# Capacity-routed mixture of experts on one core: second-layer weights by column halves, routings ended earlier, a third expert's tokens turned by DMA

## The chip, the core and the metric

The kernel runs on one core of a Trainium2 chip. The metric is the device time of one execution in microseconds (us), as the median of several runs. The core has five engines with a queue of instructions each: PE (TensorE, matmuls), DVE (VectorE), ACT (ScalarE), POOL (GpSimd) and SP (SyncE, which here issues transfers). An engine takes its instructions in the order of its queue, and one that has to wait holds up all that stand behind it.

## What is computed

The output of an attention is the input of a mixture of experts:

```python
scores = cap * np.tanh(scale * (q @ k.T) / cap)        # 8 x 12 heads, seq 448, dim 64
attn = softmax(scores); attn_out = attn @ v            # -> x: 3584 tokens x 768
logits = x @ w_gate                                    # 3584 x 8
cap = N // E                                           # 448
for idx in np.argsort(-logits.flatten()):
    tok, e = idx // E, idx % E
    if assigned[tok] >= 0 or counts[e] >= cap: continue
    assigned[tok] = e; counts[e] += 1
for e in range(E):
    mask = assigned == e
    out[mask] = np.maximum(x[mask] @ w1[e], 0.0) @ w2[e]   # 768 -> 1024 -> 768
```

All is fp32. Each expert ends with exactly 448 tokens. Which expert fills up first, and with which tokens, is known only when the logits are there, so the kernel finds it step by step: one routing for each expert.

## The kernel before

**Parts.** Attention and the first routing take the first 376 us or so. Then eight experts follow one another, in the order in which they fill up; "expert p" below means the p-th of that order, from 0. While PE works on expert p, the routing of expert p+1 or p+2 runs beside it on the other engines, in pieces.

**One expert.** The first layer (`ffn1`, f = 0 to 7) makes one block of 128 hidden columns at a time, the second (`ffn2`, u = 0 to 7) one tile of up to 128 tokens (t = u % 4) and one half of 384 output columns (hf = u // 4). The products of fp32 numbers are made from three matmuls: both factors are split into a high part (rounded) and a low part (the rest), and high x high, high x low and low x high are added. So a block of the first layer has 6 x 3 = 18 matmuls, a tile of the second has 24 (the last tile 16). That makes 144 + 176 = 320 matmuls for an expert. Each of them is one **tick**: the kernel counts them as it writes the program, and by this count it decides where all other work goes. "Tick 100 of expert 4" is behind the hundredth matmul of that expert. A call with `work={3:...}` puts its piece behind the third matmul of its block.

**The splits.** `split1(p,f)` splits a block of w1, `split2` a block of w2, both by `cut`: ACT rounds the high part (L758), POOL subtracts for the low part (L762). w1 blocks go out two blocks ahead, behind matmul 3 of a block of the first layer. Two blocks of w2 rows are loaded as one piece of 768 KB (`load2`, three buffers) and split in two column halves, one behind matmul 11 of each block of the first layer.

**The routing.** It is one Python generator; `step()` runs it to its next `yield`, and the number that is yielded says after how many ticks the next piece is written into the program. A negative number means: at that absolute tick (`LK` in `phases0`). For expert p it looks for the threshold in three searches, A, B and C (`select`): in each step, DVE (L504) and ACT (L501) count the values below several thresholds, a small matmul (L508) adds the counts over the partitions, and DVE picks the next thresholds. L567 sums the result over partitions. `finalise` turns thresholds to token lists: comparisons and a running count on DVE (L605 to L611), matmul L617 and L618 (prefix sums), one-hot patterns on DVE (L621 to L635), matmul L639, DVE again (L642, L644), matmul L647, and the list of token numbers. Its small matmuls stand in PE's queue among those of the expert, at the ticks that the yields make.

**The tokens of the next expert.** As soon as a list is there, POOL gathers the 448 rows of x from DRAM (L790). For experts 1 and 2 PE turns them, four transposes for each of six pieces (`xtr`, L806), and ACT and DVE split the result (`cutx`). From the third expert on (`FT`), DMA turns them: 26, 34, 42 and 50 ticks behind the gather, ACT rewrites a tile as two int16 planes (`planes`, L812) and sends it to DRAM, and behind the second and the fourth SP issues a DMA transpose (L816) of the first 256 and of the other 192 tokens. `cutt` splits these in four pieces: high parts on ACT (L822), low parts on DVE (L823).

**The order** is written out by hand: for every engine it is the order in which the Python code makes the calls. Nothing moves at run time.

Of the kernel before, what the change touches and what calls it, by code (L numbers as in the profile page):

```python
# [325 lines left out]
YL=[]  # L326
LK=(0,0,145,132,132,132,132,100); FT=3
ACF=1
# [4 lines left out]
class Routing:  # L333
# [188 lines left out]
    def search(s,wp,turned=()):  # L522
        nc=s.nc; v=nc.vector
# [12 lines left out]
        v.scalar_tensor_tensor(q,s.V["VA"][:,:s.NV],s.tA,vb,op0=ALU.subtract,op1=ALU.add)  # L536
        if s.cur>FT: yield max(0,306-s.place()-4)
        s.R=[]
# [62 lines left out]
    def finalise(s,wp,L,update):  # L601
        nc=s.nc; T=s.T; NC=s.NC; v=nc.vector
# [10 lines left out]
        if s.cur>=FT: s.early(s.cur,ei)  # L613
        yield 8 if s.cur==1 else 30 if s.cur==7 else 18 if s.cur>=FT else 12
        ps=s.psum()
# [19 lines left out]
        v.tensor_tensor(oi,oh,wide(s.idc),op=ALU.mult)  # L635
        yield 18
        ps=s.psum()
# [46 lines left out]

W1B=4; W2B=3
def ffn_all(nc, tc, ctx, rt, xs, xz, w1, w2, out, ident, E, wp, deferred, xctx, gen):
# [4 lines left out]
    res=rt.results  # L691
    hint=[0]; now=[0]
    def step():
        h=next(gen,0)
        hint[0]=max(-h-now[0],4) if h<0 else h
# [11 lines left out]
    m=0  # L707
# [33 lines left out]
    def load1(p,i,gate=None):  # L741
# [5 lines left out]
        raw[p,1,i]=t  # L747
    def load2(p,i,gate=None):
        if p>=E: return
        e=expert(p)  # L750
        t=ws.tile([128,2,DM],F32,name="w2r",bufs=W2B)
        if gate is not None: nc.gpsimd.tensor_copy(t[0:1,0,0:1],gate)
        nc.sync.dma_start(t,w2[bass.ds(e,1),i*256:i*256+256,:].rearrange("o (c p) d -> p (o c) d",p=128))
        raw[p,2,i]=t
    def cut(key,r,shape,name,bufs,eng=None,view=lambda t:t,use=lambda t:t):
# [8 lines left out]
    def split1(p,f,eng=None):  # L764
        if p>=E: return
        cut((p,1,f),raw[p,1,f],[128,DC,128],"w1",3,eng)
    def split2(p,hf,i):
        if p>=E: return
        r=raw[p,2,i]
        src=r[:,:,hf*HD:hf*HD+HD]  # L770
        view=use=lambda t:t.rearrange("p (o d) -> p o d",o=2)
        cut((p,2,hf,i),src,[128,2*HD],"w2",8,None,view,use)
    def early(p,ei):
# [43 lines left out]
    def cutt(p,k,c0,c1):  # L817
        newx(p)
        o,n=((0,256),(256,192))[k]
        h,l=(t[:,c0:c1,o:o+n] for t in xgT[p])  # L820
        x=xgp[k][:,c0*n:c1*n].rearrange("p (c t) -> p c t",c=c1-c0)
        nc.scalar.activation(h,x,AF.Copy)  # L822
        nc.vector.tensor_tensor(l,x,h.bitcast(F32),op=ALU.subtract)  # L823
    def cutx(p,c,ps):
        h,l=xgT[p]
# [86 lines left out]
    for p in range(E):  # L912
        lastp=p==E-1; cur[0]=p
        for f in range(FC):
            if f==0: load2(p,2)
            if f+W1B-1<FC and (p==0 or f+W1B-1>=W1B): load1(p,f+W1B-1) if (p,1,f+W1B-1) not in raw else None
            if f==(3 if p else 4): load2(p,3)
            work={}
            if f+2<FC and (p,1,f+2) not in spl: work[3]=[lambda: split1(p,f+2)]
            at={f:[(11,f%2,f//2)] for f in range(FC)}  # L920
            if p==0: at={1:[(11,0,0)],2:[(11,1,0)],3:[(11,0,1)],4:[(11,1,1)],5:[(11,0,2)],6:[(3,1,2),(11,0,3)],7:[(3,1,3)]}
            for n,hf,i in at.get(f,()): work[n]=[lambda hf=hf,i=i: split2(p,hf,i)]
            if p==1 and f==0: work[1]=[lambda: xtr(1,4)]; work[4]=[lambda: xtr(1,5)]
            ffn1(p,f,work)
# [12 lines left out]
        for u in range(8):  # L937
# [8 lines left out]
            if p<1 and u==7: wk={15:[lambda: xtr(1,3)]}  # L946
            if p+1>=FT and not lastp:
                for m,k,c in {6:[(5,0,0),(9,1,0),(12,0,3),(15,1,3)]}.get(u,()): wk[m]=wk.get(m,[])+[lambda k=k,c=c: cutt(p+1,k,c,c+3)]
            ffn2(p,u%4,u//4,(CL if p<1 else CP)[u] if p+1<FT else [],wk)
# [60 lines left out]
```

## Time and profile before

| | |
|---|---|
| time, median of 3 runs | 895.49 us (894.23 to 896.71) |
| the profiled execution's own time | 898.33 us |
| its span in the profile | 896.6 us |
| granted TensorE clock | 1.0 of full speed |
| DMA traffic | 136.84 MB |

The starts of the experts in the trace (first matmul of L855) and the time to the next one, or to the last output:

| expert | first matmul at | first matmul of L883 at | to the next expert |
|---|---|---|---|
| 1 | 448.22 | 479.49 | 66.6 |
| 2 | 514.84 | 545.13 | 62.6 |
| 3 | 577.47 | 611.35 | 66.2 |
| 4 | 643.69 | 674.79 | 63.5 |
| 5 | 707.14 | 738.28 | 62.4 |
| 6 | 769.57 | 799.29 | 62.6 |
| 7 | 832.13 | 861.32 | |

The profile's timeline has one row for each instruction: start in us from the start of the span, duration, engine, line of the code, what it writes and reads, sizes, and in brackets how long its engine sat idle before it and which instruction ended that. Where rows alike stand together it joins them ("x3"). Matmuls overlap, so the distance from one start to the next is what a matmul takes, not its duration.

### The profile page before, as it was taken

To read this page: it belongs to the slowest core of one execution; us is meant where nothing else is said; L and a number is where in the kernel's file an instruction comes from. 1 tells how busy PE (TensorE), PEld (TensorE's weight loads), DVE (VectorE), ACT (ScalarE), POOL (GpSimd) and SP (SyncE) were. 2 spreads that over 40 slices of the span, in tenths; PEclk is the share of its full clock that TensorE was granted. 3 is DMA by queue.
4 is the path that set the end of the run, shared out by engine and by line. 5 is a ranking of instruction groups with operands and counts; after the bars stand their busy time and mean duration, and the time that the engine had idled before them with its cause. 6 is when DMAs were issued, how large, how long until landed. Compare 5 with 4: busy or idle time off the path is not lost.

```text
span 896.6 us, 17418 instructions
## 1 busy us (share of the span) xinstructions
PE 862.6 (96%) x6222; PEld 631.5 (70%) x6222; DVE 613.7 (68%) x2012; ACT 584.8 (65%) x836; POOL 352.7 (39%) x506
## 2 busy tenths in 40 slices
PE   6899999999999997899999999899999999999997
PEld 3333444444333335788989989789989889989997
DVE  3788988989888888777787777677777774260210
ACT  6998898889899957274382573683673764535521
POOL 7100000000000008574584394394592683773841
PEclk9999999999999999999999999999999999999999
DMA  8799999997994007760923623944945927928701
GB/s 119 115 135 140 130 177 169 136 166 109 213 174 83 1 14 255 228 219 8 319 80 100 227 80 113 274 142 128 275 127 161 298 70 207 305 59 236 252 10 53
DMA packets 321463, 136.84 MB, mean 153 GB/s; under 512 B 252288, under 2 KB 303232, under 8 KB 320864
## 3 DMA queue, kind: packets, MB, share of 16 engines
q1 hardware_dynamic: 312304, 106.59, 54.0%
q0 software_dynamic: 4656, 22.02, 7.2%
q10 hardware_dynamic: 4416, 7.11, 2.4%
q8 instruction: 49, 0.80, 0.4%
q14 instruction: 38, 0.31, 0.1%
HBM read 97.15 MB, written 31.65 MB: 144 GB/s over the span
## 4 chain that ended last, share of the span: by engine, by line
PE 69%; issue 12%; POOL 5%; DVE 5%; DMA 4%; SPq 2%; ACT 2%; POOLq 0%; ACTq 0%; DVEq 0%
PE psH L855 20%; PE psH L883 15%; PE psA L189 12%; PE psS L148 10%; PE psM L206 4%; DMA xg<-xz 2%; PE psS L153 2%; SPq L92 2%; POOL w1l L762 2%; POOL out_dram L868 1%; DVE cmpD L504 1%; PE psM L37 1%; DVE es L165 1%; POOL xg L790 1%; DMA k<-in_k_dram 1%
## 5 line engine op out<-in xcount | busy, mean ns | idle before, releaser
L883 PE MATMUL psH<-w2h,hh 128*128 128x384 f32 x896 | 243.0, 340 | 0.0
L883 PE MATMUL psH<-w2l,hh 128*128 128x384 f32 x512 | 174.2, 340 | 0.0
L154 ACT ACTIVATE e<-psS 128x896 f32<-128x896 f32 x168 | 147.4, 909 | 30.8 <-PE psS L148 18.2
L883 PEld LDWEIGHTS psH<-w2h,hh 128*128 128x128 f32 x896 | 162.1, 188 | 0.2
L159 ACT ACTIVATE e<-e,bias 128x1792 f32<-128x1792 f32 (+2 forms) x74 | 147.3, 1991 | 2.0
L855 PE MATMUL psH<-xgh,w1h 128*128 128x448 f32 x384 | 143.4, 373 | 0.3 <-ACT xgh L827 0.3
L855 PE MATMUL psH<-xgh,w1l 128*128 128x448 f32 x384 | 141.3, 368 | 0.0
L855 PE MATMUL psH<-xgl,w1h 128*128 128x448 f32 x384 | 141.0, 368 | 0.1
L148 PE MATMUL psS<-tq,tk 64*64 64x448 f32 x1152 | 129.6, 544 | 7.8 <-DVE tq L133 3.5
L189 PE MATMUL psA<-e,nv 64*64 64x448 f32 x1104 | 120.3, 539 | 1.2 <-DVE xT L199 1.2
L762 POOL TENSOR_TENSOR w2l<-w2r,w2h 128x768 fp32r<-128x768 f32 x64 | 118.1, 1846 | 6.8 <-ACT w2h L758 6.5
L762 POOL TENSOR_TENSOR w1l<-w1r,w1h 128x768 fp32r<-128x768 f32 x62 | 114.4, 1847 | 15.7 <-ACT w1h L758 10.9
L460 POOL TENSOR_SCALAR r_Bt<-r_b 112x4 f16<-112x4 int32 x1 | 0.2, 199 | 303.5 <-DVE rin L243 303.5
L165 DVE TENSOR_TENSOR es<-es,e 64x896 f32<-64x896 f32 (+2 forms) x74 | 100.4, 1356 | 2.6 <-ACT e L159 1.3
L883 PEld LDWEIGHTS psH<-w2l,hh 128*128 128x128 f32 x512 | 96.4, 188 | 0.0
L148 PEld LDWEIGHTS psS<-tq,tk 64*64 64x64 f32 x1152 | 43.4, 132 | 73.9 <-issue 37.6
L889 ACT ACTIVATE on<-psH 128x384 f32<-128x384 f32 x48 | 23.4, 488 | 100.3 <-PE psH L883 93.8
L189 PEld LDWEIGHTS psA<-e,nv 64*64 64x64 f32 x1104 | 46.0, 133 | 59.2 <-issue 50.1
L863 DVE SCALAR_TENSOR_TENSOR hh<-psH,hh 128x64 fp32r<-128x64 f32 (+1 forms) x128 | 43.9, 384 | 58.6 <-ACT hh L861 56.7
L868 POOL DMA_INDIRECT out_dram<-on,idx x31 | 34.4, 1110 | 117.8 <-ACT on L889 87.7
L861 ACT ACTIVATE hh<-psH 128x448 fp32r<-128x448 f32 x64 | 34.8, 543 | 65.6 <-PE psH L855 54.9
L855 PEld LDWEIGHTS psH<-xgh,w1h 128*128 128x128 f32 x384 | 72.6, 189 | 5.5 <-ACT xgh L827 0.5
(337 smaller groups left out, 1363.5 us busy)
## 6 DMA issues: line engine op xcount, KB each, us to landing
w1r<-in_moe_w_dram SPq DMA_DIRECT2D x64, 384.0 KB
w2r<-in_moe_w_dram SPq DMA_DIRECT2D x32, 768.0 KB
k<-in_k_dram SPq DMA_DIRECT2D x92, 112.0 KB
q<-in_q_dram SPq DMA_DIRECT2D x92, 112.0 KB
nv<-in_v_dram SPq DMA_DIRECT2D x72, 128.0 KB
xz<-pl ACTq DMA_DIRECT2D x15, 384.0 KB
xs<-xn SPq DMA_DIRECT2D x4, 1344.0 KB
xs<-xn SPq DMA_DIRECT2D x4, 896.0 KB
```

Source lines behind the costliest of these rows:

```text
L148: for c in range(2): nc.tensor.matmul(ps[c*64:c*64+64,h,:S],tks[g,0][hp,o,u*128+c*64:u*128+c*64+64],tks[g,1][hp,o,:],start=True,stop=True)
L154: nc.scalar.activation(ev(g,r),ps[:,:,:S],AF.Tanh,scale=sr[0])
L159: act=lambda: nc.scalar.activation(e,e,AF.Exp,scale=sr[1],bias=bias)
L165: t=es_t[g]; add=lambda o,a,b: nc.vector.tensor_tensor(o,a,b,op=ALU.add)
L189: nc.tensor.matmul(avp[g,o][h*64:h*64+64,:S],lhs,rhs[hp,h,:],start=(j==0 and x==0),stop=j==3)
L206: nc.tensor.matmul(ps[g*32:g*32+32,:S],lhs,rhs,start=first,stop=last)
L762: (eng or nc.gpsimd).tensor_tensor(view(l),r,view(h).bitcast(F32),op=ALU.subtract)
L855: nc.tensor.matmul(ps[:,:C],a[:,c,:],b[:,c,:],start=(m==0),stop=(m==DC*3-1)); m+=1
L861: nc.scalar.activation(h[:,:C],ps[:,:C],AF.Relu)
L863: nc.vector.scalar_tensor_tensor(h[:,d:d+b-a],ps[:,a:b],0.0,h[:,a:b].bitcast(F32),op0=ALU.max,op1=ALU.subtract)
L868: st=nc.gpsimd.indirect_dma_start(out=dst,out_offset=bass.IndirectOffsetOnAxis(ap=ix,axis=0),in_=src,in_offset=None)
L883: nc.tensor.matmul(ps[:,:HD],h[:,f,a:a+128],spl[p,2,hf,f//2][w][:,f%2,:],start=(m==0),stop=(m==nm-1))
```

## The change

1. `FT` goes from 3 to 2: expert 2's tokens are turned by DMA as those of the later experts, and are split by `cutt`; its first two blocks of w1 are loaded from `early` too.
2. The absolute ticks `LK` at which `finalise` may start become 100 for all routings from the second on (before 145, 132 and, for the last, 100), a wait between the searches A and B goes, and the yields ahead of L617 and L639 (now L616 and L638) become 10 and 16 (before 12, 18 or 30, and 18). As a result the last small matmul (L647, now L646) moves from tick 188 of expert 1 to 184, from 176 of experts 2 to 5 to 166, 148, 134 and 134, and from 156 of expert 6 to 134.
3. w2 is loaded by column halves: pieces of 384 KB, six buffers. From expert 2 on, the loads go out at f = 0 to 5. From expert 3 to 6, five splits stand in the first layer (f = 0 to 4) and the last three in the second layer (u = 2 and 3).
4. The four `cutt` pieces of the next expert stand at other places: behind matmuls 4 and 14 of u = 5 and u = 6 (before: 5, 9, 12 and 15 of u = 6), for expert 2 behind 1, 8 and 18 of u = 6 and 4 of u = 7. Each of them delays the next piece of the routing by 5 ticks, unless the routing is waiting for its absolute tick.

What moves in the queues is seen best at three places. The first is DVE, as expert 3 starts (`xgl` are the low parts of its x, from the first and second transposed half, `xg_4110` and `xg_4111`; `cmpD` are the comparisons of search B, whose sums L508 waits for). Before:

```order
L512 SCALAR_TENSOR_TENSOR fl,th<-psR,r_H8A 128x4
L536 SCALAR_TENSOR_TENSOR r_qt<-r_VAt,th,psV 128x224
L823 TENSOR_TENSOR xgl<-xg_4110,xgh 128x3x256
L823 TENSOR_TENSOR xgl<-xg_4111,xgh 128x3x192
L823 TENSOR_TENSOR xgl<-xg_4110,xgh 128x3x256
L823 TENSOR_TENSOR xgl<-xg_4111,xgh 128x3x192
L504 TENSOR_SCALAR cmpD,r_ce_309<-r_qt,r_T8B 128x224 x5
L541 TENSOR_SCALAR jk,tot<-th,r_zero 128x1
```

and now:

```order
L821 TENSOR_TENSOR xgl<-xg_4110,xgh 128x3x256 x2
L512 SCALAR_TENSOR_TENSOR fl,th<-psR,r_H8A 128x4
L536 SCALAR_TENSOR_TENSOR r_qt<-r_VAt,th,psV 128x224
L821 TENSOR_TENSOR xgl<-xg_4111,xgh 128x3x192
L504 TENSOR_SCALAR cmpD,r_ce_309<-r_qt,r_T8B 128x224 x5
L540 TENSOR_SCALAR jk,tot<-th,r_zero 128x1
L821 TENSOR_TENSOR xgl<-xg_4111,xgh 128x3x192
L512 SCALAR_TENSOR_TENSOR fl,th<-psR,r_H8B 128x8
```

The two low parts of the first half have moved ahead of the end of search A (L512), and one of the second half behind the comparisons. One of the second half still stands ahead of them.

The second place is POOL in expert 5, around the gather of expert 6 (`w1l`, `w2l` are the low parts of the splits). Before:

```order
L762 TENSOR_TENSOR w2l_8093<-w2r_7915,w2h_8092 128x768
L760 MEMSET gap_4109 1x1
L762 TENSOR_TENSOR w2l_8167<-w2r_7915,w2h_8166 128x768
L790 DMA xg0_4110<-xs_60,idx_8248 128x768 x2
L790 DMA xg1_4111<-xs_60,idx_8248 128x768
```

and now:

```order
L762 TENSOR_TENSOR w1l_8102<-w1r_8030,w1h_8101 128x768
L788 DMA xg0_4110<-xs_60,idx_8207 128x768 x2
L788 DMA xg1_4111<-xs_60,idx_8207 128x768
L788 DMA xg1_4111<-xs_60,idx_8207 64x768
L760 MEMSET gap_4109 1x1
L762 TENSOR_TENSOR w2l_8366<-w2r_7965,w2h_8365 128x768
L760 MEMSET gap_4109 1x1
L762 TENSOR_TENSOR w2l_8381<-w2r_8028,w2h_8380 128x768
```

The gather has moved ahead of the last splits of w2; it stands right behind the last split of w1.

The third is DVE in expert 6, where the routing of expert 7 begins its `finalise` (`hh` is the hidden layer, one pair of rows for each block of the first layer). Before:

```order
L605 TENSOR_SCALAR gt_9532<-qq_9181,wB_9177 112x32
L606 TENSOR_SCALAR gteq_9533<-qq_9181,wB_9177 112x32
L607 SCALAR_TENSOR_TENSOR gteq_9533<-r_kk_341,e8s_9179,gt_9532 112x32
L609 SCALAR_TENSOR_TENSOR scan_9537<-r_ones64_173,gteq_9533 112x64
L611 TENSOR_SCALAR ei_9539<-e8s_9179 1x1
L863 SCALAR_TENSOR_TENSOR hh_9343<-psH_9516,hh_9343 128x64
L863 SCALAR_TENSOR_TENSOR hh_9343<-psH_9516,hh_9343 128x384
L863 SCALAR_TENSOR_TENSOR hh_9343<-psH_9570,hh_9343 128x64
L863 SCALAR_TENSOR_TENSOR hh_9343<-psH_9570,hh_9343 128x384
L621 SCALAR_TENSOR_TENSOR pG_9605<-scan_9537,psR_9602,gteq_9533 112x32
```

and now:

```order
L604 TENSOR_SCALAR gt_9572<-qq_9154,wB_9150 112x32
L605 TENSOR_SCALAR gteq_9573<-qq_9154,wB_9150 112x32
L606 SCALAR_TENSOR_TENSOR gteq_9573<-r_kk_341,e8s_9152,gt_9572 112x32
L608 SCALAR_TENSOR_TENSOR scan_9577<-r_ones64_173,gteq_9573 112x64
L610 TENSOR_SCALAR ei_9579<-e8s_9152 1x1
L862 SCALAR_TENSOR_TENSOR hh_9375<-psH_9556,hh_9375 128x64
L862 SCALAR_TENSOR_TENSOR hh_9375<-psH_9556,hh_9375 128x384
L620 SCALAR_TENSOR_TENSOR pG_9611<-scan_9577,psR_9608,gteq_9573 112x32
```

Between the scan and the operations behind L617 (now L616), one block of the first layer instead of two is left.

The diff (`...` marks what is left out):

```diff
@@ -324,7 +324,7 @@
 
 
 YL=[]
-LK=(0,0,145,132,132,132,132,100); FT=3
+LK=(0,0,100,100,100,100,100,100); FT=2
 ACF=1
 LF=1
 TA=0
@@ -534,7 +534,6 @@
         vb,vc=s.vps[:,:s.NV],s.vps[:,s.NV:2*s.NV]
         if s.cur==0: s.warm(WT)
         v.scalar_tensor_tensor(q,s.V["VA"][:,:s.NV],s.tA,vb,op0=ALU.subtract,op1=ALU.add)
-        if s.cur>FT: yield max(0,306-s.place()-4)
         s.R=[]
         def total(a,b):
             t=wp.tile([128,1],F32,name="tot",bufs=4); jk=wp.tile([128,1],F32,name="jk",bufs=2)
@@ -611,7 +610,7 @@
         v.tensor_scalar(ei,s.e8s[0:1],-1.0,8.0,op0=ALU.mult,op1=ALU.add)
         s.ei=ei
         if s.cur>=FT: s.early(s.cur,ei)
-        yield 8 if s.cur==1 else 30 if s.cur==7 else 18 if s.cur>=FT else 12
+        yield 8 if s.cur==1 else 10
         ps=s.psum()
         warm=(lambda n: s.warm(n)) if s.cur==0 else (lambda n: None)
         nc.tensor.matmul(ps[:112,0:2],s.lo,sc[:,:,NC-1],start=True,stop=False)
@@ -633,7 +632,7 @@
         v.tensor_tensor(oh,s.ihi,wide(hi[:,0,:]),op=ALU.is_equal)
         oi=wp.tile([112,G,16,8],F16,name="oi",bufs=1)
         v.tensor_tensor(oi,oh,wide(s.idc),op=ALU.mult)
-        yield 18
+        yield 16
         ps=s.psum()
         for g in range(G):
             nc.tensor.matmul(ps[:,:224].rearrange("p (j k) -> p j k",k=8),oi[:,g].rearrange("p r k -> p (r k)"),oj[:,:,g*8:g*8+8],start=(g==0),stop=(g==G-1))
@@ -682,16 +681,16 @@
             yield from s.finalise(wp,L,p<s.E-1)
 
 
-W1B=4; W2B=3
+W1B=4; W2B=6
 def ffn_all(nc, tc, ctx, rt, xs, xz, w1, w2, out, ident, E, wp, deferred, xctx, gen):
     C=448; DM=768; DC=6; DF=1024; FC=8; HD=384
     TS=[(0,128),(128,128),(256,128),(384,64)]
     ws=ctx.enter_context(tc.tile_pool(name="ws",bufs=3))
     pt=rt.pp
     res=rt.results
-    hint=[0]; now=[0]
+    hint=[0]; now=[0]; lk=[False]
     def step():
-        h=next(gen,0)
+        h=next(gen,0); lk[0]=h<0
         hint[0]=max(-h-now[0],4) if h<0 else h
     ET=mybir.EngineType
     late=[]
@@ -745,13 +744,14 @@
         if gate is not None: nc.gpsimd.tensor_copy(t[0:1,0,0:1],gate)
         nc.sync.dma_start(t,w1[bass.ds(e,1),:,i*128:i*128+128].rearrange("o (c p) f -> p (o c) f",p=128))
         raw[p,1,i]=t
-    def load2(p,i,gate=None):
+    order=lambda p: [(i%2,i//2) if p==E-1 else (i//4,i%4) for i in range(2*FC//2)]
+    def load2(p,n,gate=None):
         if p>=E: return
-        e=expert(p)
-        t=ws.tile([128,2,DM],F32,name="w2r",bufs=W2B)
+        e=expert(p); hf,i=order(p)[n]
+        t=ws.tile([128,2,HD],F32,name="w2r",bufs=W2B)
         if gate is not None: nc.gpsimd.tensor_copy(t[0:1,0,0:1],gate)
-        nc.sync.dma_start(t,w2[bass.ds(e,1),i*256:i*256+256,:].rearrange("o (c p) d -> p (o c) d",p=128))
-        raw[p,2,i]=t
+        nc.sync.dma_start(t,w2[bass.ds(e,1),i*256:i*256+256,hf*HD:hf*HD+HD].rearrange("o (c p) d -> p (o c) d",p=128))
+        raw[p,2,hf,i]=t
     def cut(key,r,shape,name,bufs,eng=None,view=lambda t:t,use=lambda t:t):
         h=ws.tile(shape,F32R,name=name+"h",bufs=bufs)
         l=ws.tile(shape,F32R,name=name+"l",bufs=bufs)
@@ -764,12 +764,10 @@
     def split1(p,f,eng=None):
         if p>=E: return
         cut((p,1,f),raw[p,1,f],[128,DC,128],"w1",3,eng)
-    def split2(p,hf,i):
-        if p>=E: return
-        r=raw[p,2,i]
-        src=r[:,:,hf*HD:hf*HD+HD]
+    def split2(p,n):
+        hf,i=order(p)[n]
         view=use=lambda t:t.rearrange("p (o d) -> p o d",o=2)
-        cut((p,2,hf,i),src,[128,2*HD],"w2",8,None,view,use)
+        cut((p,2,hf,i),raw[p,2,hf,i],[128,2*HD],"w2",8,None,view,use)
     def early(p,ei):
         ereg[p]=nc.sync.value_load(ei[0:1,0:1],min_val=0,max_val=E-1)
         for i in range(2): load1(p,i)
@@ -821,6 +819,7 @@
         x=xgp[k][:,c0*n:c1*n].rearrange("p (c t) -> p c t",c=c1-c0)
         nc.scalar.activation(h,x,AF.Copy)
         nc.vector.tensor_tensor(l,x,h.bitcast(F32),op=ALU.subtract)
+        if not lk[0]: cnt[0]-=5
     def cutx(p,c,ps):
         h,l=xgT[p]
         src=ps[:,:C]
@@ -912,14 +911,12 @@
     for p in range(E):
         lastp=p==E-1; cur[0]=p
         for f in range(FC):
-            if f==0: load2(p,2)
+            for n in ((2,3),(4,),(5,),(6,),(7,),(),(),())[f] if p==0 else ((2,),(3,),(4,),(5,),(6,),(7,),(),())[f]: load2(p,n)
             if f+W1B-1<FC and (p==0 or f+W1B-1>=W1B): load1(p,f+W1B-1) if (p,1,f+W1B-1) not in raw else None
-            if f==(3 if p else 4): load2(p,3)
             work={}
             if f+2<FC and (p,1,f+2) not in spl: work[3]=[lambda: split1(p,f+2)]
-            at={f:[(11,f%2,f//2)] for f in range(FC)}
-            if p==0: at={1:[(11,0,0)],2:[(11,1,0)],3:[(11,0,1)],4:[(11,1,1)],5:[(11,0,2)],6:[(3,1,2),(11,0,3)],7:[(3,1,3)]}
-            for n,hf,i in at.get(f,()): work[n]=[lambda hf=hf,i=i: split2(p,hf,i)]
+            at={0:{1:[(11,0)],2:[(11,1)],3:[(11,2)],4:[(11,3)],5:[(11,4)],6:[(3,5),(11,6)],7:[(3,7)]},1:{k:[(11,k)] for k in range(FC)},2:{**{k:[(11,k)] for k in range(6)},6:[(8,6)]},E-1:{k:[(11,k)] for k in range(FC)}}.get(p,{k:[(11,k)] for k in range(5)})
+            for m,n in at.get(f,()): work[m]=[lambda n=n: split2(p,n)]
             if p==1 and f==0: work[1]=[lambda: xtr(1,4)]; work[4]=[lambda: xtr(1,5)]
             ffn1(p,f,work)
         if lastp:
@@ -944,8 +941,10 @@
             if u==7: load2(p+1,1)
             wk=({5:{14:[lambda: split1(p+1,0)]},6:{8:[lambda: split1(p+1,1)]}} if p+1<FT else {5:{2:[lambda: split1(p+1,0)],12:[lambda: split1(p+1,1)]}}).get(u,{})
             if p<1 and u==7: wk={15:[lambda: xtr(1,3)]}
-            if p+1>=FT and not lastp:
-                for m,k,c in {6:[(5,0,0),(9,1,0),(12,0,3),(15,1,3)]}.get(u,()): wk[m]=wk.get(m,[])+[lambda k=k,c=c: cutt(p+1,k,c,c+3)]
+            if p>1:
+                for m,n in ({3:[(2,7)]} if p==2 else {2:[(2,5),(12,6)],3:[(2,7)]}).get(u,()): wk[m]=wk.get(m,[])+[lambda n=n: split2(p,n)]
+            if p+1>=FT:
+                for m,k,c in ({6:[(1,0,0),(8,0,3),(18,1,0)],7:[(4,1,3)]} if p+1==FT else {5:[(4,0,0),(14,0,3)],6:[(4,1,0),(14,1,3)]}).get(u,()): wk[m]=wk.get(m,[])+[lambda k=k,c=c: cutt(p+1,k,c,c+3)]
             ffn2(p,u%4,u//4,(CL if p<1 else CP)[u] if p+1<FT else [],wk)
             if u>3: pend.append((p,u%4))
 
```

## The prediction

> **What bounds the kernel now.** I read the page first, then who waits for whom on PE from 380 us on (the expert part; columns: total us, times, longest), then PE's timeline at each wait, then the engine named there. From the page, and from the view of waits:
>
> ```profile
> PE 862.6 (96%) x6222; PEld 631.5 (70%) x6222; DVE 613.7 (68%) x2012; ACT 584.8 (65%) x836; POOL 352.7 (39%) x506
> ```
> ```profile
> PE psR L508 <- DVE cmpD L504: 4.3, 4, 3.0
> PE psR L639 <- DVE oi L635: 1.6, 1, 1.6
> ```
>
> PE is the bound. In the expert part it never waits for weights; it waits for the small matmuls of the routing, which stand in its queue at fixed places and come too early for DVE. An edit can only win by shortening those waits or by taking work off PE. PE's timeline (start, duration, in brackets idle time and its releaser) gives their size from start to start:
>
> ```profile
> 577.47 0.36 PE L855 MATMUL psH<-xgh,w1h 128*128 128x448 f32 x1
> 577.94 0.47 PE L855 MATMUL psH<-xgl,w1h 128*128 128x448 f32 x1
> 581.38 0.18 PE L508 MATMUL psR<-r_ce,r_bo 128*128 128x8 bf16 x1 [2.97 <-DVE cmpD L504]
> ...
> 643.69 0.37 PE L855 MATMUL psH<-xgh,w1h 128*128 128x448 f32 x1
> 643.90 0.37 PE L855 MATMUL psH<-xgl,w1h 128*128 128x448 f32 x1
> 644.83 0.18 PE L508 MATMUL psR<-r_ce,r_bo 128*128 128x8 bf16 x1 [0.56 <-DVE cmpD L504]
> ...
> 795.73 0.37 PE L855 MATMUL psH<-xgh,w1h 128*128 128x448 f32 x1
> 796.29 0.16 PE L617 MATMUL psR<-scan,r_lo 112*112 112x2 f16 x1 [0.20 <-DVE ei L611]
> ...
> 799.82 0.34 PE L883 MATMUL psH<-w2h,hh 128*128 128x384 f32 x1
> 801.74 0.56 PE L639 MATMUL psR<-oj,oi 112*128 112x224 f16 x4 [1.58 <-DVE oi L635]
> ```
>
> A first-layer matmul takes 0.21 us (643.69 to 643.90), one of the second layer 0.18 (below). Above that, PE loses 0.26 + 3.23 us as expert 3 starts, 0.72 as expert 4 starts, 0.7 as expert 5 starts (4.3 in the view of waits, less 2.97 and 0.56, for it and one more), 0.35 + 1.74 in expert 6: **7.0 us**. The cause at the starts is the x of the next expert. DVE's low parts of x (L823) stand ahead of its compares and wait for ACT's high parts (L822), and these for the DMA transpose:
>
> ```profile
> 551.31 0.19 PE L647 MATMUL psR<-ev,r_sel 128*128 128x28 f16 x1
> ...
> 576.40 1.99 ACT L822 ACTIVATE xgh<-xg 128x576 fp32r<-128x576 f32 x3 [4.45 <-DMA xg<-xz]
> ...
> 577.12 2.37 DVE L823 TENSOR_TENSOR xgl<-xg,xgh 128x576 fp32r<-128x576 f32 x3 [4.01 <-ACT xgh L822]
> ...
> 680.98 0.19 PE L647 MATMUL psR<-ev,r_sel 128*128 128x28 f16 x1
> ...
> 703.30 0.69 ACT L822 ACTIVATE xgh<-xg 128x576 fp32r<-128x576 f32 x1 [1.68 <-DMA xg<-xz]
> ```
>
> From the last matmul of a routing (L647) to the landing of the second half of x pass 22.3 us (680.98 to 703.30) to 25.1 us (551.31 to 576.40). From L647 to the first matmul of expert 3 (551.31 to 577.47) pass 26.16 us for 144 ticks, 0.18 each.
>
> **What goes.** The x of expert 2 no longer takes 24 transposes in PE's queue:
>
> ```profile
> 502.79 0.60 PE L806 MATMUL psX<-ident,xg 128*128 128x128 f32 x4
> 503.14 0.60 PE L883 MATMUL psH<-w2h,hh 128*128 128x384 f32 x2
> ```
>
> Four of them push PE by 0.35 us (502.79 to 503.14); six pieces make **2.1 us**. If all waits above went too, the change would win 9.1 us.
>
> **What comes at the starts of experts 2 and 3.** L646 (L647 of before) now stands at tick 184 of expert 1, 166 of expert 2, 148 of expert 3 and 134 afterwards (before: 188, then 176).
>
> Expert 1 to 2: eight ticks later than tick 176, so 26.2 - 8 x 0.18 = 24.8 us to expert 2; the compare matmul stands ten ticks in, at 26.8. Its operand is ready at the landing + 0.69 (cut on ACT) + two low parts of 0.79 (a third of 2.37) + the compares, 1.9 (579.49, the end of the low parts, to 581.38), and 0.4 for L536: landing + 4.6 = 26.9 to 29.7. PE waits 0.1 to 2.9; at the middle landing, 23.6, it is **1.4**. This wait is new.
>
> Expert 2 to 3: 26.2 + 10 x 0.18 = 27.9 to expert 3, and L508 stands eleven ticks before that, at 26.0. One low part now stands behind the five compares, so ready = landing + 0.69 + 0.79 + 1.9 = 25.7 to 28.5: 0 to 2.5, in the middle **0.9**, in place of 3.5.
>
> Experts 4 to 7: cuts at ticks 260 to 294 come at least 136 ticks, 24 us, after L646 for the second half, and the compares stand before or 23 ticks behind them. I take **0** and lose the waits of 0.7 there.
>
> **What comes at the end of the routings.** L616 now stands 10 ticks behind the start of finalise (before 12, 18 and 30), L638 16 further on. In experts 1 to 3 it is only 14 ticks behind the sum over partitions (L566, L567 of before). The expert 1 of before shows that chain:
>
> ```profile
> 479.85 0.28 PE L567 MATMUL psR<-R,r_onesf 128*112 128x16 f32 x2
> ...
> 482.48 0.29 DVE L609 TENSOR_TENSOR_SCAN scan<-r_ones,gteq 112x64 f16<-112x64 f16 x1
> ```
>
> It took 2.9 us (479.85 to 482.77). Fourteen ticks are 2.6 us in expert 1, in the second layer, and 2.9 in experts 2 and 3, with first-layer matmuls among them: 0.3 + 0.1 + 0.1 = **0.5**.
>
> In experts 4 to 6 finalise will start at tick 100, amid POOL's splits, as in expert 6 of before. There PE's first matmul and the one of tick 110 stand at
>
> ```profile
> 769.57 0.36 PE L855 MATMUL psH<-xgh,w1h 128*128 128x448 f32 x1
> ...
> 791.88 0.36 PE L855 MATMUL psH<-xgh,w1l 128*128 128x448 f32 x1
> ```
>
> the first and the eleventh split on POOL, and the group of ACT's part of a split, at
>
> ```profile
> 773.34 1.86 POOL L762 TENSOR_TENSOR w1l<-w1r,w1h 128x768 fp32r<-128x768 f32 x1
> ...
> 792.41 1.83 POOL L762 TENSOR_TENSOR w1l<-w1r,w1h 128x768 fp32r<-128x768 f32 x1
> ```
> ```profile
> L758 ACT ACTIVATE w1h<-w1r 128x768 fp32r<-128x768 f32 x62 | 51.3, 836 | 3.0 <-DMA w1r<-in_moe_w_dram 3.0
> ```
>
> and on DVE the first and the last operation ahead of L617 at
>
> ```profile
> 789.21 1.41 DVE L605 TENSOR_SCALAR gt<-qq,wB 112x32 f32<-112x32 f32 x1
> ...
> 794.33 1.90 DVE L609 TENSOR_TENSOR_SCAN scan<-r_ones,gteq 112x64 f16<-112x64 f16 x1
> ```
>
> The scan takes 0.29 us in expert 1, behind the splits, and 1.90 in expert 6, till POOL's split ends; gt and the two operations between are held in the same way. The change leaves eleven splits ahead of finalise instead of fourteen (5 of w2, 6 of w1). In expert 6 of before they run from 773.34, 3.8 us after PE's first matmul at 769.57, and the eleventh is the row at 792.41, which ends at 794.24. The first split is called at tick 3, 0.6 us in, and ACT's part takes 0.84: at the earliest it starts 1.5 us in. The change's x has landed earlier, so ACT and the scatter ahead of the first split are freer; I take 2.3, nearer to that end. Then the eleventh ends at 2.3 + 11 x 1.84 = 22.5. DVE reaches gt at +19.6 (789.21), loses the rest of the tenth and all of the eleventh, and has the scan at +23.1. L616 stands at tick 110, +22.3 (791.88): a wait of 0.8; with the start as measured 2.8. In experts 4 and 5 the compares slow PE and ticks come later, the burst too; no row shows the overlap, so I take the nearest, expert 6: 0.9 each, 0 to 2.8. Three experts make **2.7**.
>
> **What I cost at nothing.** A half load of w2 is as large as a load of w1, for which PE never waits; each is issued 47 ticks (9 us) ahead of its split, and as a split frees its buffer a half earlier, SP is not held longer. If that cover went, a late split would stop PE at w2l in the second layer. The last split of w2 goes out at tick 218 and is read at 250: 32 x 0.18 = 5.8 us against 0.84 + 1.84 for its two parts; hidden. The four cuts of x for expert 2 and the four int16 planes ahead of them take the place of six cuts on ACT and lie in its idle time.
>
> **Sum.** -7.0 - 2.1 + 1.4 + 0.9 + 2.7 + 0.5 = -3.6 us against the profiled execution of 898.33 us (span 896.6). That lies 2.8 over the median of the three timed runs, 895.49, so I take the difference from the median: **891.9 us**. With every new wait at its low end it is -9.1 + 0.1 + 0.5 = -8.5 and 887.0; with all at the high end (2.9 + 2.5 + 8.4 + 0.5) +5.2 and 900.7.
>
> **Rivals.** *All new waits are covered*: the landing comes at 22.3 and the burst of splits is through by tick 100: **887.0**. For it: the landing of 22.3 did occur. Against: eleven splits need 20.2 us of POOL by themselves, and tick 100 lies at 20.3.
>
> *Late landing.* The second half lands at 25.1 at both starts, as at expert 3's of before: 2.9 + 2.5 instead of 2.3, **895.0**, no measurable change.
>
> *The burst holds the whole chain* (slower). In experts 4, 5 and 6 each operation of the chain is caught by a split of its own, as in expert 6 now, where gt starts 2.7 us before tick 110 and the scan ends 4.3 behind it (789.21, 791.88, 796.23). L616 then waits 4.3 us, three times 12.9 instead of 2.7: **902.1**. It decides from the burst's end: three waits of 2.1 eat the gain, and those come from a burst that ends 1.5 us behind tick 110. For it: the first split at +3.8 as measured. Against: only eleven splits are left ahead.
>
> *Cuts of x against splits of w1.* From expert 3 on, splits of w1 go out at ticks 258 and 268 and low parts of x at 260 and 270, both inputs in SBUF like those of the chain above. Held to the split's end (tick 283; with a scatter ahead of it on POOL 287), then 0.79 + 0.5 + 1.9 us, 18 ticks, the compares are ready at tick 301 to 305; L508 stands at 307. So nothing by these ticks, but with half a microsecond more of delay on POOL about 0.5 us at each of four starts: **893.9**.
>
> The Trainium skill, "SBUF — State Buffer", section "Who interferes with whom", says that a VectorE instruction with two SBUF inputs contends with a GpSimd one that reads SBUF, and that the one issued first keeps the port for its whole length. The scan's rows agree (1.90 against 0.29). By that rule this rival holds the low parts, and the sum would be -1.6; by the ticks alone it is -3.6.
>
> *It doesn't do what it says.* Finalise can't start at tick 100 where the search is longer: in experts 1 to 3 L616 stands at ticks 160, 142 and 124, as the search allows. Then the starts of experts 2 and 3 stay: that is in the sum.
>
> **Chances.** Forecast 0.42 (its own spread 889.5 to 894.3), covered 0.20, late landing 0.13, cuts against splits 0.10, burst 0.15. Within 0.3%, about what a measurement of this kernel can tell from no change, means 892.8 to 898.2. Three quarters of the forecast lie below it, and the covered case: 0.51 faster. The rest of the forecast, the late landing and the cuts: 0.34. Slower: the burst, 0.15. The range 886.5 to 898.0 holds the first four cases with some tenths beside their ends and leaves out the burst, where two or three experts are held.
>
> **What would show it.** Right: no L806 for expert 2; waits of PE for cmpD of 0 to 3 us at the starts of experts 2 and 3 and none at 4 to 7; waits at L616 of about 1 us in experts 4 to 6, with gt and gteq at 1 to 2 us on DVE beside POOL's L762. Wrong: waits at L616 of 4 us; waits for w2l; waits of PE for xgl or xgh of over 1 us; a second transpose that lands later than 25 us after L646.

## The result and the profile after

The changed kernel took 900.63 us (median of 5 runs, 899.40 to 903.62) against 895.49 (5 runs, 894.23 to 896.71): ratio 1.0062, 95% interval 1.0039 to 1.0085. It is **slower by about 0.6%**; 891.9 was forecast, with 898.0 as the upper end. The profiled execution took 900.70 us, its span is 898.9. The medians differ by 5.1 us and the spans by 2.3, since the profiled execution of before lay 2.8 over its median and this one lies at it. What follows explains the 2.3; what the other 2.8 consist of, no trace shows.

The page's line of engines, and below it the view of who waits for whom on PE from 380 us on (total us, times, longest), of the changed kernel:

```profile
PE 860.7 (96%) x6198; PEld 628.3 (70%) x6198; DVE 620.5 (69%) x2016; ACT 587.6 (65%) x832; POOL 351.9 (39%) x507
```
```profile
PE psR L508 <- DVE cmpD L504: 2.6, 3, 1.9
PE psR L616 <- DVE ei L610: 2.4, 3, 1.2
PE psH L882 <- DVE wA L593: 1.5, 1, 1.5
PE psH L882 <- DVE hh L862: 1.2, 1, 1.2
PE psR L508 <- ACT xgh L820: 0.9, 1, 0.9
PE psR L508 <- ACT cmpA L501: 0.8, 1, 0.8
...
PE psH L882 <- POOL w2l L762: 0.3, 1, 0.3
```

PE works 1.9 us less (24 transposes are gone), and the span is 2.3 us longer. The waits of before are smaller or gone, but there are now waits in places where PE had none: in the second layer, for the hidden layer (`hh`, and, by its last semaphore, `wA`), for ACT and for w2. From PE's timeline, taken from start to start as in the prediction (steps over 0.35 us, less the step of a matmul), the stops of experts 1 to 6 add up to 7.0 us before and 11.9 after: 4.9 more, less 2.1 for the transposes, makes 2.8; the span shows 2.3.

**The hidden layer.** DVE's timeline as expert 4 goes from the first to the second layer, and PE's beside it:

```profile
675.51 0.43 DVE L665 TENSOR_TENSOR L<-L,pen 112x256 f32<-112x256 f32 x1
675.97 0.42 DVE L444 TENSOR_REDUCE r_m<-L 112x32 f32<-112x256 f32 x1
...
679.90 0.19 DVE L468 SCALAR_TENSOR_TENSOR r_K<-r_kk,r_Ct 112x32 f32<-112x32 f16 x1
680.00 0.69 DVE L862 SCALAR_TENSOR_TENSOR hh<-psH,hh 128x64 fp32r<-128x64 f32 x2
```
```profile
679.18 0.34 PE L882 MATMUL psH<-w2h,hh 128*128 128x384 f32 x1
680.74 0.44 PE L882 MATMUL psH<-w2h,hh 128*128 128x384 f32 x1 [1.22 <-DVE hh L862]
```

With the list of tokens at tick 134, the routing's next step, propose (L444 to L468), is written into the program at tick 144, ahead of the last block of the hidden layer. ACT's part of that block ends at 676.28 (L860 at 675.73, 0.55 us), DVE's starts 3.7 us later, behind propose, and the first tile of the second layer needs it: 1.38 us (679.18 to 680.74, less 0.18), and 1.70 in expert 5. Before, propose came 42 ticks later, in the second layer.

**The low parts of x.** POOL, DVE and PE at the end of expert 3:

```profile
633.37 1.87 POOL L762 TENSOR_TENSOR w1l<-w1r,w1h 128x768 fp32r<-128x768 f32 x1 [0.55 <-ACT w1h L758]
...
635.22 2.54 POOL L762 TENSOR_TENSOR w1l<-w1r,w1h 128x768 fp32r<-128x768 f32 x1
```
```profile
634.05 4.52 DVE L821 TENSOR_TENSOR xgl<-xg,xgh 128x768 fp32r<-128x768 f32 x2 [1.00 <-ACT xgh L820]
638.50 0.15 DVE L512 SCALAR_TENSOR_TENSOR fl<-psR,r_H8B 128x8 f32<-128x8 f32 x1
```
```profile
640.82 0.18 PE L508 MATMUL psR<-r_ce,r_bo 128*128 128x8 bf16 x1 [0.92 <-ACT xgh L820]
```

Two low parts, 0.95 us each when alone, take 4.52 beside two splits of POOL: the first 2.00, the second 2.60. The step of the search behind them (L512) starts at 638.50, though its sum had left PE at 635.09, its compares end at 640.75, and PE stops for 1.09 us (the view names ACT; the compares of DVE end last). Expert 4 ends in the same way with a stop of 0.69.

Expert 2 ends with a stop of 2.07. There too a low part is held (567.47 to 571.36), but what ends last is the landing of x. ACT and DVE wait for the second transposed half behind it:

```profile
572.97 0.69 ACT L820 ACTIVATE xgh<-xg 128x576 fp32r<-128x576 f32 x1 [3.05 <-DMA xg<-xz]
```
```profile
573.69 0.76 DVE L821 TENSOR_TENSOR xgl<-xg,xgh 128x576 fp32r<-128x576 f32 x1 [0.90 <-ACT xgh L820]
```

It landed 25.1 us behind L646, and the compares follow it.

### The profile page after: what moved, and what is told of

Same layout as the page of the kernel before. It is cut to its first block, busy times and chain, and to the rows that moved or that the text cites. A ratio compares the mean times of both kernels' runs of the same rounds, so it can differ in the third digit from the quotient of the medians.

```text
span 898.9 us, 17533 instructions
## 1 busy us (share of the span) xinstructions
PE 860.7 (96%) x6198; PEld 628.3 (70%) x6198; DVE 620.5 (69%) x2016; ACT 587.6 (65%) x832; POOL 351.9 (39%) x507
## 4 chain that ended last, share of the span: by engine, by line
PE 62%; issue 14%; DVE 9%; POOL 4%; DMA 4%; ACT 3%; SPq 2%; POOLq 0%; ACTq 0%; DVEq 0%
PE psH L854 19%; PE psA L189 12%; PE psH L882 11%; PE psS L148 10%; PE psM L206 4%; PE psS L153 2%; SPq L92 2%; DVE es L165 1%; POOL out_dram L867 1%; DVE cmpD L504 1%; DMA xg<-xs,idx 1%; PE psM L37 1%; POOL xg L788 1%; DMA xg<-xz 1%; DMA k<-in_k_dram 1%
## 5 line engine op out<-in xcount | busy, mean ns | idle before, releaser
L860 ACT ACTIVATE hh<-psH 128x448 fp32r<-128x448 f32 x64 | 34.8, 543 | 84.4 <-PE psH L854 80.2
L854 PEld LDWEIGHTS psH<-xgh,w1l 128*128 128x128 f32 x384 | 72.3, 188 | 5.2
```

Source lines behind the costliest of these rows:

```text
L854: nc.tensor.matmul(ps[:,:C],a[:,c,:],b[:,c,:],start=(m==0),stop=(m==DC*3-1)); m+=1
L860: nc.scalar.activation(h[:,:C],ps[:,:C],AF.Relu)
```

## The experiments

The kernel before took 898.6 to 898.9 us (medians) beside these runs, 3 us more than in its first five, so only ratios to it are compared.

**e1: the kernel before once more.**

> The kernel before, unchanged, for a second trace. Theory 1 (the waits of before that the prediction counted as removable, 7.0 us, come from one profiled execution that was 2.8 us over the median): the start of expert 3 loses clearly less than 3.5 us here, the sum is near 4 us, and the span is near 894. Theory 2 (those waits are there in every execution): 3.5 and 7.0 us again, a span near 896.6. The ratio to before is 1.000 in both, within 0.003.

Ratio 0.9994 (0.9970 to 1.0018), span 897.8. Expert 3 starts with a stop of 0.83 us instead of 3.49, but experts 4 and 5 with 1.28 and 1.79, and L639 waits 2.6: 6.8 in all. Theory 2 for the sum, theory 1 for each single stop: the landings of x vary, and with them the places of these stops.

**e2: propose behind the hidden layer.**

```diff
-            yield 9
+            yield 12 if s.cur in (5,6) else 9
```

> The change, with three ticks more ahead of the next routing's propose in experts 4 and 5 (12 instead of 9), so that DVE makes the last block of the hidden layer ahead of propose and not behind it. Theory 1 (PE's stops of 1.38 and 1.70 us behind the start of the second layer of experts 4 and 5, which the trace puts down to hh and to wA, both come from propose's 5 us ahead of that block on DVE): both stops go, about 3 us less than the change, 897.5 us. Theory 2 (the second is a wait for the memset wA, as named): only the first goes, 899.2. Theory 3 (PE stops there for something else, such as w2): no difference, 900.6.

Ratio 1.0002 (0.9984 to 1.0020). Both stops are gone, in expert 5 too, where `wA` was named: theory 1. The ratio falls by 4 to 5 us where the two stops make 3.1; the intervals allow that. DVE's timeline of e2 shows the order turned round:

```profile
675.01 0.69 DVE L862 SCALAR_TENSOR_TENSOR hh<-psH,hh 128x64 fp32r<-128x64 f32 x2 [0.40 <-ACT hh L860]
675.61 0.41 DVE L444 TENSOR_REDUCE r_m<-L 112x32 f32<-112x256 f32 x1
```

**e3: splits of w1 apart from the low parts.**

```diff
-... else {5:{2:[lambda: split1(p+1,0)],12:[lambda: split1(p+1,1)]}}
+... else {4:{2:[lambda: split1(p+1,0)],12:[lambda: split1(p+1,1)]}}
```

> The change, with the first two splits of the next expert's w1 in u = 4 instead of u = 5, so that POOL is through with them before DVE takes the low parts of x. Theory 1 (POOL's splits hold the low parts, which took 4.0 to 4.8 us for two instead of 1.7, and with them the compares): low parts of 0.75 to 1.1 us everywhere, the stops of PE for L508 at the ends of experts 3 and 4 (1.09 and 0.69 us) go and that of expert 2 (2.07) falls to what the late landing leaves; 2 to 3 us less than the change, 898 us. Theory 2 (the landing of the transpose is what is late): the low parts may be shorter, but the stops stay, 900.6.

Ratio 0.9998 (0.9981 to 1.0015). The groups of low parts by shape, of the changed kernel and of e3 (busy us, mean ns):

```profile
L821 DVE TENSOR_TENSOR xgl<-xg,xgh 128x768 fp32r<-128x768 f32 x12 | 25.5, 2158 | 14.3 <-ACT w1h L758 10.2 <-ACT xgh L820 4.1
```
```profile
L821 DVE TENSOR_TENSOR xgl<-xg,xgh 128x768 fp32r<-128x768 f32 x12 | 12.0, 1039 | 11.2 <-ACT xgh L820 11.2
```

The mean is halved, and the stops at the ends of experts 3 and 4 are gone: theory 1. L616 in expert 4 also waits 0.39 us instead of 1.37. The stop at the end of expert 2 is gone too, but there x landed 22.0 us behind L646 instead of 25.1, which is theory 2's cause. The other traces say the same: with landings of 25.1 and 24.8 (the change, e5) that stop is 2.07 and 1.73 us, with 24.0 (e2) 0.95, and with the splits of w1 moved it is 0 for 22.0 (e3), 22.1 (e13) and 23.6 (e7), but 2.4 and 1.9 for 25.6 (e12) and 25.2 (e14). In e4 it is 1.08 with a landing of 22.5 and the low part held for 3.61 us, so the hold can stop PE there as well.

In return expert 2 of e3 starts with stops of 1.24 + 0.59 + 0.90 us; the second half of its x landed 25.5 us behind L646 instead of 22.4.

**e4: finalise at tick 132.**

```diff
-LK=(0,0,100,100,100,100,100,100)
+LK=(0,0,100,100,100,132,132,132)
```

> The change, with finalise of the routings in experts 4 to 6 from tick 132 on instead of 100. Theory 1 (the early end costs twice: L616 waits behind POOL's splits, 1.37 + 0.20 + 1.16 us, and propose comes ahead of the hidden layer, 1.38 + 1.70): all five go, 5 to 6 us less than the change, about 895. Theory 2 (the early end pays by an earlier x, and the losses come from the splits in the second layer): no gain or a loss, since x lands 32 ticks later and DVE and ACT meet more work in the second layer: 900 to 903.

Ratio 1.0103 (1.0070 to 1.0135): theory 2 by its direction, and somewhat beyond its price. The stops at L616 and for the hidden layer are gone, but w2 comes too late in the second layer. PE in expert 4 of e4:

```profile
694.38 0.62 PE L882 MATMUL psH<-w2h,hh 128*128 128x384 f32 x2 [0.19 <-ACT w2h L758]
696.27 0.44 PE L882 MATMUL psH<-w2l,hh 128*128 128x384 f32 x1 [1.28 <-POOL w2l L762]
```

ACT's parts of the three late splits alternate here with the four int16 planes of 1.47 us (683.88 to 692.93), and POOL's follow. With the splits where they are, the late end costs more than the early one.

**e5: the changed kernel once more; e6: L616 six ticks later.**

> The changed kernel, unchanged, beside the next three on one chip. If the chip of the first experiments only measures everything higher, the ratio to before is 1.006 again; if the change's loss was small and that of its first five runs too large, it is 1.002 to 1.004. In the trace: stops of PE behind the start of the second layer of experts 4 and 5 of 1.4 to 1.7 us, low parts of x of up to 4.4 us, as in its first trace.

Ratio 1.0051 (1.0030 to 1.0072): the loss is real on other runs, and the interval leaves open which of the two sizes. Stops for the hidden layer of 1.37 and 1.39 us, at L616 of 1.36, 0.21 and 1.13, at the ends of experts 2 to 4 of 1.72, 1.06 and 0.68.

```diff
-        yield 8 if s.cur==1 else 10
+        yield 8 if s.cur==1 else 16 if s.cur>=5 else 10
```

> The change, with L616 16 ticks behind the start of finalise in experts 4 to 6 instead of 10; the list and the next propose come six ticks later too. Theory 1 (L616 is early by at most 1.4 us, seven ticks, and propose then comes behind the hidden layer): the stops at L616 in experts 4 to 6 (1.37 + 0.20 + 1.16 us) and the two stops for the hidden layer (1.38 + 1.70) go: 5 to 6 us less than the change, 2 to 3 less than the kernel with propose alone moved. Theory 2 (POOL's splits hold DVE as long as they run, and six ticks only move the wait on to L638, or to the splits of w2 in the second layer): the sum of the waits stays, no difference against the kernel with propose alone moved.

Ratio 1.0029 (1.0014 to 1.0045): between the theories. The stops at L616 in experts 4 and 6 and those for the hidden layer are gone. In expert 5 L616 still waits 1.1 us, and a low part is now held so that expert 4 ends with a stop of 2.94 us in place of 0.69:

```profile
696.08 4.38 DVE L821 TENSOR_TENSOR xgl<-xg,xgh 128x768 fp32r<-128x768 f32 x1 [1.14 <-ACT xgh L820]
```

**e7: both, L616 later and splits of w1 in u = 4.**

> The change, with L616 six ticks later as above and the splits of w1 in u = 4. If the three losses add up (hidden layer 3.1, L616 2.7, low parts about 2.5 us): 8 us less than the change, ratio to before 0.997, and the waits left are those of ACT's compares and w2's low parts in the second layer of experts 2 and 3 (1.4 us) and of late landings at expert 2. If they don't add up (the next wait takes their place): no better than each alone, ratio 1.000.

Ratio 0.9979 (0.9962 to 0.9997). The losses add up, but for stops of 3.3 us at the start of expert 2, as in e3.

**e8: all splits of w2 in the first layer.**

```diff
-            at={0:{...},1:{...},2:{...},E-1:{...}}.get(p,{k:[(11,k)] for k in range(5)})
+            at={0:{...}}.get(p,{k:[(11,k)] for k in range(FC)})
...
-            if p>1:
-                for m,n in ({3:[(2,7)]} if p==2 else {2:[(2,5),(12,6)],3:[(2,7)]}).get(u,()): ...
```

> The change, with all eight splits of w2 in the first layer of every expert, as before the change. Theory 1 (splits in the second layer cost: ACT's compares and w2's low parts late in experts 2 and 3, 1.4 us, while a few splits more ahead of L616 change little): 1 to 2 us less than the change. Theory 2 (fourteen splits instead of eleven push the chain ahead of L616 and L638 in experts 4 to 6, as in expert 6 of before): waits there of 2 to 4 us in each, 3 to 6 us more than the change.

Ratio 1.0333 (1.0312 to 1.0353): theory 2, and far beyond its price. DVE and PE in expert 4 of e8:

```profile
666.38 6.13 DVE L590 SCALAR_TENSOR_TENSOR qq<-r_K,wA,r_K 112x32 f32<-112x32 f32 x1
```
```profile
673.89 0.16 PE L616 MATMUL psR<-scan,r_lo 112*112 112x2 f16 x1 [4.81 <-DVE ei L610]
```

An operation that takes 0.24 us at its shortest in the changed kernel is held for 6.13 us, to the end of a split and through three more (POOL's rows run from 665.20 to 672.46 without a pause), and everything behind it on DVE is late. In expert 5 the same operation is held for 9.52 us, in expert 6 L604 for 6.73, and each time PE's clock falls too (below). With the end at tick 100, then, the three splits have to leave the first layer.

**e9: e7 with expert 2's x turned by PE.**

```diff
-... FT=2
+... FT=3
```

with the comparisons of search A and the places of the cuts kept as they are in the change.

> The kernel with the three moves, with expert 2's x turned by PE as before the change (the cuts of the later experts stay where the change has them). Theory 1 (DMA for expert 2 pays: it saves 2.1 us of PE and costs a stop of 0 to 3.3 us at expert 2's start, according to the landing): about even with the kernel with the three moves, 0.997 to 1.000, and the start of expert 2 free of stops in the trace while 24 transposes stand in PE's queue. Theory 2 (the planes and transposes for expert 2 also cost elsewhere, in the second layer of expert 1): 1 to 2 us faster than the three moves.

Ratio 1.0011 (0.9994 to 1.0028): neither. It is slower than e7, by 0.0032, and the start of expert 2 has no stop; but the routings move with `FT`, and new stops stand in the experts behind: L616 in expert 2 (1.7 us), ACT's compares (1.5), the hidden layer of expert 3 (1.4). What DMA for expert 2 is worth by itself stays open.

**e10 and e11: parts of the change on the kernel before.** e11 is the kernel before with half loads alone (`W2B=6`, `load2` and `split2` as changed); e10 has `FT=2` as well, with the four cuts at their old places.

> The kernel before with two parts of the change alone: half loads of w2 and expert 2's x by DMA (all splits of w2 in the first layer, routings and cuts where they were). If the DMA of expert 2's x pays by itself: 2.1 us of transposes gone, a stop of 0 to 3 us at its start, ratio 0.998 to 1.001. If it costs more than it saves, 1.002 to 1.005, and it is part of the change's loss.

> The kernel before with half loads of w2 alone. If the loads cost nothing, as the prediction has it: 1.000 within 0.002, no wait for w2 on PE. If the shorter rows of the halves slow the queue of transfers (and so the landings of x): 1.002 or more, and landings later than 25 us behind L646.

e10: 1.0035 (1.0017 to 1.0053), e11: 1.0023 (0.9997 to 1.0049). In e10 the first low part of expert 2 still waits for its x (DVE idle for 3.75 us until ACT's high part), the compares of search A behind them stop PE for 3.8 us in expert 1 (at 511.79), so the new places of the cuts belong to this part. In e11 no wait for w2 is seen and no x lands later than 24.4 us behind L647; the verdict is open. Its trace has, as before, the stops at the starts of experts 3 to 5, and one of 3.2 us at L617 in expert 6. Fourteen splits stand ahead there, as before the change, where the same stop was 0.35. This time the first operation of the chain didn't get through between them:

```profile
789.54 7.64 DVE L605 TENSOR_SCALAR gt<-qq,wB 112x32 f32<-112x32 f32 x1
```

**e12: e7 with the late splits of w2 called earlier in experts 2 and 3** (tick 172; 160, 169 and 218), and L616 six ticks later still in expert 5.

> The kernel with the three moves; the late splits of w2 called earlier in experts 2 and 3 (ACT's part ahead of the int16 planes), and L616 six ticks later still in expert 5. If w2's low parts and ACT's compares in experts 2 and 3 are late because the planes and the splits meet on ACT: their stops, 1.03 and 1.13 us, and that at L616 in expert 5, 1.09, go: 3 us less than the three moves, ratio 0.994 to 0.996. If POOL's gather holds the splits anyway, the stop for w2l in expert 2 stays.

Ratio 1.0027 (1.0011 to 1.0043): slower than e7. The three stops are gone, but expert 2 ends with one of 2.4 us that e7 doesn't have (its x landed at 25.6 us, in e7 at 23.6), and the two early splits in expert 3 now run on POOL without a pause while DVE is in propose:

```profile
620.01 4.33 DVE L461 TENSOR_SCALAR r_Ct<-r_c 112x32 f16<-112x32 int32 x1
...
620.61 1.86 POOL L762 TENSOR_TENSOR w2l<-w2r,w2h 128x768 fp32r<-128x768 f32 x1
...
622.44 1.86 POOL L762 TENSOR_TENSOR w2l<-w2r,w2h 128x768 fp32r<-128x768 f32 x1
...
626.79 0.17 PE L508 MATMUL psR<-r_cd,r_bo 128*128 128x4 bf16 x1 [2.82 <-DVE cmpD L504]
```

0.18 us of work become 4.33, and the next compare matmul stops PE for 3.0.

**e13 and e14: the two losses out and nothing else; e7 with expert 1 left alone.** e13 is e2 and e3 together, e14 is e7, both with the splits of w1 in u = 4 only from expert 2 on:

```diff
+... else {4:{2:[lambda: split1(p+1,0)],12:[lambda: split1(p+1,1)]}} if p>1 else {5:{...}}
```

> The change with its two unforeseen losses taken out and nothing else: propose three ticks later in experts 4 and 5, and the splits of w1 in u = 4 from expert 2 on (in expert 1 they stay in u = 5, since with them in u = 4 the second half of expert 2's x landed 25.3 to 26.1 us behind L646 in three traces and 22.4 to 24.2 in six others). If the two losses are what made the change slower and they add: 3.1 us (hidden layer) and 3 to 4 us (low parts, at the ends of experts 2 to 4), 6 to 7 us under the change, ratio to before 0.997 to 0.999. If each only covers the other, or the next wait comes up: 1.000 or more.

> The kernel with the three moves, with expert 1's splits of w1 back in u = 5. If the later landing at expert 2 came from that move: the stops at its start fall from 3.3 us to 0 to 1.5 and the ratio from 0.998 to 0.995 to 0.997. If the landing varies by itself: the same 0.998, and a landing of over 25 us in this trace too.

e13: 895.14 us, 0.9961 (0.9943 to 0.9980). e14: 894.65 us, 0.9955 (0.9943 to 0.9967). Both beat both kernels. The view of waits on PE from 380 us on, of e13:

```profile
PE psR L616 <- DVE ei L610: 1.4, 3, 1.0
PE psR L508 <- DVE cmpD L504: 0.9, 3, 0.4
PE psR L508 <- ACT cmpA L501: 0.9, 1, 0.9
```

The two losses add up: from 1.0062 and 1.0051 to 0.9961 is 8 to 9 us, more than the 6 to 7 expected. e14 comes out as its first theory has it, with 1.5 us of stops at the start of expert 2. Expert 2's x landed at 22.8 and 24.1 us, within the range of the six traces with expert 1 unmoved (22.4 to 24.2), against 25.3 to 26.1 in the three with it moved. But in e10, where expert 1's splits are unmoved too and L646 stands four ticks later, it landed at 25.1. So the later landing goes with the move in expert 1 in these traces; that the move causes it, and by which transfers, isn't shown.

## Why the prediction was wrong

**What bounds the kernel** was read rightly, and the 7.0 us of waits too: 6.8 in e1. **The transposes** and the removed waits at the starts of experts 3 to 5 and at L639 went as said.

**The start of expert 2**, 1.4 us, between 0.1 and 2.9: 0.1 in the first trace, 1.5 in e5, 2.7 and 3.3 where w1 was moved. With w1 unmoved (the change, e2, e4, e5, e6, e8) the landings are 22.4 to 24.2 us, within the bounds of 22.3 and 25.1; those of e3, e7 and e12 (25.3 to 26.1) lie beyond.

**The end of expert 2**, 0.9 us (its terms give 1.0), between 0 and 2.5: 2.07, by the mechanism named. The landing of 25.1 was the upper bound itself. That the early one at the start of expert 2 offsets the late one at its end is luck: -1.4 and +1.2 us.

**The end of the routings**, 2.7 + 0.5 us: 1.37 + 0.20 + 1.16 in experts 4 to 6, 0.32 in expert 1. The sum is right, and the cause: DVE's chain beside POOL's splits. How it is held was priced otherwise, to the end of the one split that each operation falls on. In expert 4 L590 was held through a change of splits (2.54 us at 664.02), and in expert 6 `gt` (3.15 at 792.56), so that the sum comes out so near is in part luck. The burst that was to hold the whole chain did not come, but e8 shows how near it is: three splits more, and it is there at 5 us an expert.

**Two steps failed.** The larger is a term that the prediction doesn't have, and so puts at nothing: what else moves with L646 on DVE. The prediction followed the gather, the planes and the transposes, but not propose, ten ticks behind, which lands on the border of the two layers and holds the hidden layer: 3.1 us, and e2, which moves propose alone, has neither stop. What stands behind a moved step moves too; this was followed for the transfers and not for DVE.

The other is "Experts 4 to 7 ... I take 0 and lose the waits of 0.7 there". The waits at the starts went, but the low parts at ticks 260 and 270 met the splits of w1 at 258 and 268, as the rival "cuts of x against splits of w1" had it, with a chance of 0.10. PE stopped for 1.09 and 0.69 us at the ends of experts 3 and 4. The rival held the low parts to tick 283 or, behind a scatter, 287, and so left L508 at 307 free. In expert 3 the second split ends at 637.76, 2.4 us behind tick 283 (635.38): ACT began the first split's high part 1.5 us behind its tick (632.46 against 630.91), and the second split itself took 2.54 us beside the low part instead of 1.84. In expert 4 it ends 1.8 us behind that tick.

Taking out either loss (e2, e3) brings the time back to that of before, and both together (e13) below it. The rule of the Trainium skill that stood beside this rival ("SBUF — State Buffer", section "Who interferes with whom") agrees: the low part, with two inputs in SBUF, took 2158 ns in the mean beside the splits and 1039 with them moved. That it is the port, the traces don't show by themselves. That the wait can go on into the second split, as the 4.38 us of e6 show, is more than the rule was read to say.

**"What I cost at nothing"** was wrong in size: the splits in the second layer stop PE for 0.43 us in expert 2 (w2l at 563.99) and 1.0 in expert 3 (ACT's compares behind them and the planes, 627.36). A wait for w2l was one of the signs named for being wrong; a landing later than 25 us, at the end of expert 2, was another. The cover named, 5.8 us, was one of time between call and use; on ACT it is filled by the planes, as e4 shows.

In numbers: forecast -7.0 - 2.1 + 5.5; measured in the trace, -2.1 + 4.9 for all stops, so 11.9 us of new or remaining stops instead of 5.5. Of the 6.4 us between them, 3.1 are the hidden layer, 1.8 the ends of experts 3 and 4, 1.4 the second-layer splits, and 1.2 the late landing at expert 2's end (2.07 instead of 0.9); 0.5 is a compare in expert 1; 1.4 at expert 2's start and 0.2 at L616 come off.

## What to carry to other kernels

When a step is moved in a hand-written order, follow every instruction that moves with it to its new neighbours, on each engine, and above all across a border where another engine waits (here the last hidden block). A short vector operation that falls on a train of GpSimd operations can cost the rest of the train, not its own length; moving the train away from it (e3) helped. One memset already stands between any two of these splits and doesn't prevent it; a longer pause was not tried.

Two traces of one kernel show which of its stops can be trusted. Those behind a landing change: 3.49 and 0.83 us at one place of the kernel before, 0.1 and 1.5 at the start of expert 2 of the change. Most of those that the order of the engines makes come again: 1.37 and 1.36 at L616 in expert 4, 1.38 and 1.37 for the hidden layer there, 1.09 and 1.06 at the end of expert 3. Not all do: L639 of before waits 1.7 and 2.6.

## What the runs showed of the hardware

**A held operation of DVE often doesn't get its turn between two of POOL.** L590 took 6.13 and 9.52 us (e8), L605 7.64 (e11), L461 4.33 (e12) and a low part 4.38 (e6), where they take 0.24, 0.23, 0.18 and 0.95 alone; POOL's rows show two to six splits following one another beside them. The Trainium skill, in the section named above, has the one that issues first keep the port for its whole length; that the waiting one stays held across the change from one split to the next, only these rows show. It isn't always so: in the profile before, the small operations of expert 6 were each held to the next split's end only (L605 1.41, at the place where it took 7.64 in e11), and so was the first low part at the end of expert 3 of the change (2.00). What decides it, these runs don't show.

**After most long stops PE runs at half its clock for 3.4 us.** The stretches of e11 around its stop of 3.2 us at L617 (busy PE, PEld, DVE, ACT, POOL; granted clock; DMA share; GB/s):

```profile
796.00:799.50 3.50, 0.43 (x3) 0.18 (x2) 3.47 (x6) 0.93 (x2) 2.93 (x3) 1.00 0.00 0
799.50:803.00 3.50, 3.49 (x11) 3.14 (x11) 3.30 (x12) 0.00 (x0) 0.00 (x0) 0.51 0.36 109
803.00:806.00 3.00, 3.00 (x19) 2.76 (x19) 1.13 (x4) 0.55 (x1) 0.00 (x0) 1.00 0.49 135
```

The nine matmuls of the first layer behind the stop take 3.42 us (799.63 to 803.05) where 9 x 0.207 = 1.86 would do, so the stop costs 1.6 us more than its length. The same follows the stops of 4.81 (e8), 3.60 (e10), 2.82 (e12), 2.79 (e6) and even 2.42 (e1, at L639); after the 2.97 of the kernel before, at 581.38, the clock stayed at 1.00. That may be why e1's span is 1.2 us longer than that of the first trace, though its stops add up to no more. What decides it, these runs don't show.
